# Rounds in groups of four, convolution four heads at a time, PSUM as one ring of single banks

## The chip, the core and the metric

One core of a Trainium2 chip runs the kernel as one launch. The metric is the device time in microseconds (us); three runs of the kernel before took 529.02 to 529.27 us, with a median of 529.07. The engines are called as in the profile: PE (TensorE, matmuls), PEld (its weight loads), DVE (VectorE), ACT (ScalarE), POOL (GpSimd) and SP (SyncE, here only an issuer of DMAs). In this kernel PE writes to PSUM, used as eight banks of 512 fp32 columns by 128 partitions, and results leave it through ACT or DVE.

## What is computed

```python
# x: (8, 3904, 192), weight: (8 heads, 7 taps)
w = softmax(weight, axis=-1)
x_pad = concat([zeros(8, 6, 192), x], axis=1)
conv[b, s, h, g] = sum_k w[h, k] * x_pad[b, s + k, h * 24 + g]
t = conv.reshape(31232, 192)
out = ((t @ w1) * (t @ w2)) @ w3 @ w_out     # 192 -> 1024 -> 1024 -> 192
```

## The kernel before, in words

The tokens are split into two streams of 15616 (four batches each, `r` = 0 and 1), which are worked on side by side: half of the 128 partitions holds stream 0, the other half stream 1. Work goes through three stages.

**Convolution** (`conv`, L261). Tokens come in windows of 64 rows, of which 58 are new; a *block* is a set of windows, `SIZES` = 10, 10, 10, 32, then five of 36 and one of 30. `load_x` (L89) brings a block to SBUF by POOL's DMAs. For each of eight heads four matmuls on quarters of the array (64x64, one for each half block and stream) multiply by a band matrix of the taps and write a pair of PSUM banks, one for each stream. DVE or ACT casts the pair to bf16 into `convo` (L295); heads 2 and 5 cross a border of 64 channels and take two casts. `store` (L299) writes the finished block to a DRAM buffer `rows` by SP's DMAs.

**First product** (`first_product`, L369). A *round* R is 512 tokens of each stream; there are 31, the last of them 256 wide. `transposes` (L345) brings a round from `rows` to SBUF, channels on partitions, with three transposing DMAs on SP, into `xT`, a ring of four rounds. For each of eight steps `ft` PE makes `pa` = t @ w1 and `pb` = t @ w2 for 128 of the 1024 columns, six matmuls of 64 rows by 512 columns each, which run two at a time; each fills a pair of banks. ACT casts `pa` to `asb` (L388), and DVE multiplies it with `pb` into `abT` (L389).

**Second product** (`second_product`, L394). W = w3 @ w_out is made once, in the prologue. For a round and a stream, 32 matmuls (four groups of 128 tokens, eight accumulation steps) multiply `abT` by W into one pair of banks `ops`; ACT copies it in one piece to `osb` (L410), one of five buffers of the tag `slot`, and SP issues the output DMA (L414).

PSUM is a pool of four tiles of two banks each (`banks`, L66), handed out in turn. The order on each engine is the order of the program text (`manual_schedule`): each engine and each DMA queue takes its instructions in that order and waits where data or a buffer isn't ready. SP's queue holds the stores, the transposes and the outputs in one line.

The prologue (up to L519) makes the weights, convolves blocks 0 to 3, runs the first products of rounds 0 to 2, and issues the transposes of rounds 3 to 6 (L515). Then come *phases* (L522): phase 0 has no first product, each later one has two rounds of them, and then second products trail: phase p does those of two rounds that were finished earlier (`LAG` = 2). Each phase convolves half a block of four heads in two places, two heads after its first second product and two at its end, and then sends the transposes of two more rounds:

```python
for i in range(done, last):
    second_product(i, 0)
    if b < NB and i == done:
        conv_two(b, 4 * e, (V, V))
    second_product(i, 1, i == NR - 1)
done = last
if b < NB:
    conv_two(b, 4 * e + 2, (V, V))
send(min(NR - 1, LAG + 2 * p + 4))
```

The last phase makes the first products of rounds 29 and 30 and all second products that are left.

Of the kernel before, what the change touches and what calls it, by code (L numbers as in the profile page):

```python
# [8 lines left out]
FP32 = mybir.dt.float32  # L9
# [7 lines left out]
def kernel(  # L17
# [19 lines left out]
    NS = 2  # L37
    TS = B * S // NS
    CH = 512
    NR = -(-TS // CH)  # L40
    RING = 4 * CH
    LAG = 2
    Q = 64
    ST = Q - PAD
    NP = D // Q
# [13 lines left out]
    const = ctx.enter_context(tc.tile_pool(name="const", bufs=1))  # L59
    stage = ctx.enter_context(tc.tile_pool(name="stage", bufs=2))  # L60
    work = ctx.enter_context(tc.tile_pool(name="work", bufs=2))
    psum = ctx.enter_context(tc.tile_pool(name="psum", bufs=4, space=bass.MemoryType.PSUM))
    dram = ctx.enter_context(tc.tile_pool(name="dram", bufs=1, space=bass.MemoryType.DRAM))
    ctx.enter_context(tc.manual_schedule())

    def banks(name):  # L66
        return psum.tile([128, NS, CH], FP32, tag="banks", name=name)

    def banks_bf16(name):
        return psum.tile([128, 16, 128], BF16, tag="banks", name=name)  # L70

    def slot(shape, dtype, name):
        return stage.tile(shape, dtype, tag="slot", bufs=5, name=name)
# [15 lines left out]
    def load_x(b, parts=(0, 1), streams=(0, 1)):  # L89
        tiles = xb_of.setdefault(b, [])  # L90
        zeros_of = zero_rows.setdefault(b, [])
        for i0, n in [v for e, v in enumerate(halves_of(b)) if e in parts]:
            if i0 == 0 and tiles:
                xb = tiles[0][0]
            else:
                xb = work.tile([128, n, D], BF16, tag="xb", bufs=6, name="xb")
            w = 0
            if i0 == 0:
                if not tiles:
                    nc.vector.memset(xb[:, 0, :], 0.0)  # L100
                for r in streams:
                    nc.gpsimd.dma_start(out=xb[Q * r:Q * r + Q, 1:n, :], in_=x_spans(r, 1, n - 1))  # L102
                w = n
            while w < n:
                i = i0 + w
                m = min(n - w, WB - i % WB)
                at_end = i + m == NWIN
                if at_end:
                    m -= 1
                if m:  # L110
                    for r in range(NS):
                        nc.gpsimd.dma_start(out=xb[Q * r:Q * r + Q, w:w + m, :],  # L112
                                            in_=x_spans(r, i, m))
                if i % WB == 0:
                    zeros_of += [(xb, 0, w), (xb, 1, w)]
                w += m
                if at_end:
                    nc.gpsimd.memset(xb[Q:128, w, :], 0.0)
                    t = tok(NWIN - 1) - PAD
                    nc.gpsimd.dma_start(out=xb[0:Q, w, :], in_=x_rows[t:t + Q, :])  # L120
                    nc.gpsimd.dma_start(out=xb[Q:Q + PAD + LAST, w, :],
                                        in_=x_rows[TS + t:TS + t + PAD + LAST, :])
                    w += 1
            if tiles and i0 == 0:
                continue
            if len(halves_of(b)) == 1:
                tiles += [(xb, 0), (xb, SIZES[b] // 2)]
            else:
                tiles.append((xb, 0))
# [61 lines left out]
    load_w(WC[1], WC[3])  # L191

    def warm(n, t=None):
        t = banks("warm") if t is None else t
        for j in range(n):
            nc.tensor.matmul(t[:, j % 2, :], zeros[:, 0:128], zeros, start=True, stop=True)  # L196

# [12 lines left out]
    nc.vector.reciprocal(out=wsum, in_=wsum)  # L210
    nc.vector.tensor_tensor(
        out=wrow, in0=wall, in1=wsum.unsqueeze(2).to_broadcast([1, H, K]), op=ALU.mult)
    wbc = banks("wbc")
    wbc = wbc[:, 0, 0:H * K // 2].rearrange("p (g e k) -> p g e k", g=2, e=2)
    wrow = wrow.rearrange("p (g a e) k -> p g a e k", g=2, a=2)
    for a in range(2):
# [20 lines left out]
        return c  # L237

    def band_sum(g, c, f):
        bps = banks("bps")  # L240
        for v, lhsT in enumerate((ident, swapped)):
            out = bps[:, 0, v * 128:v * 128 + 128].rearrange("p (e s) -> p e s", e=2)
            for k in range(K):
                nc.tensor.matmul(out, lhsT, c[:, :, k, :], start=(k == 0), stop=(k == K - 1))
        f(out=Aband[:, g].rearrange("p v e s -> p (v e s)"), in_=bps[:, 0, 0:256])
# [12 lines left out]
            c0, n = c0 + m, n - m  # L258
        return out

    def conv(b, h0, nh, evict=None, lead=0):  # L261
        n = SIZES[b] // 2
        if h0 == 0:
            convo_of[b] = work.tile([128, n, NP, NS, Q], BF16, tag="convo", bufs=2, name="convo")
        convo = convo_of[b]
        cps = banks("cps")
        warm(lead, cps)
        wd = nh * G

# [20 lines left out]
            del xb_of[b]  # L290
        if evict == ():
            return moves
        for e, (dst, part) in enumerate(moves):
            f = evict or [nc.scalar.copy]
            f[e % len(f)](out=dst, in_=part)  # L295
# [28 lines left out]
    def pe_transpose(b, k, lead=0):  # L324
        n = SIZES[b] // 2
        convo = convo_of[b]
        tps = banks_bf16("tps")
        for w in range(lead):
            nc.tensor.transpose(out=tps[:, w % 2, :], in_=zeros[:, 0:128], identity=ident)
        for w in range(n):  # L330
            nc.tensor.transpose(  # L331
                out=tps[:, w, :],
                in_=convo[:, w, k].rearrange("p r g -> p (r g)"), identity=ident)
        t0 = tok(FIRST[b])
        dst = xT[k][:, t0:t0 + 2 * n * ST].rearrange("p (c w s) -> p c w s", c=2, w=n)
        src = tps[:, 0:n, :].rearrange("p w (c s) -> p c w s", c=2)
        return dst, src[:, :, :, 0:ST]
# [30 lines left out]

    def first_product(R, between=None):  # L369
        N = width(R)  # L370
        ab = work.tile([128, JT, NS, CH], BF16, tag="abT", bufs=LAG + 1, name="abT")
        abT_of[R] = ab
        r0 = (R * CH) % RING
        for ft in range(JT):
            pq = []
            for i in range(2):
                p = banks("pa" if i == 0 else "pb")
                pq.append(p)
                for k in range(NP):
                    for r in range(NS):  # L380
# [10 lines left out]
            if between and ft in between:  # L391
                between[ft]()

    def second_product(R, r, split=False):  # L394
        ab = abT_of[R]
        ng = width(R) // 128
        t0 = r * TS + R * CH
        parts = [(g, g + 1) for g in range(ng)] if split else [(0, ng)]
        for e, (g0, g1) in enumerate(parts):
            m = g1 - g0  # L400
            ops = banks("ops")
            for g in range(m):
                for jt in range(JT):
                    nc.tensor.matmul(  # L404
                        ops[:, g // 2, (g % 2) * D:(g % 2) * D + D],
                        ab[:, jt, r, (g0 + g) * 128:(g0 + g + 1) * 128], W_sb[:, jt, :],
                        start=(jt == 0), stop=(jt == JT - 1))
            osb = slot([128, m, D], FP32, "osb")
            n = min(m, 2)
            (nc.vector.tensor_copy if split and e == 0 else nc.scalar.copy)(  # L410
                out=osb.rearrange("p (a g) d -> p a (g d)", g=n),
                in_=ops[:, 0:m // n, 0:n * D])
            t = t0 + g0 * 128
            (nc.scalar if split and g1 == ng else nc.sync).dma_start(  # L414
                out=out[t:t + m * 128, :].rearrange("(g p) d -> p g d", p=128), in_=osb)
        if r == 1:
            del abT_of[R]

# [13 lines left out]

    def w3_transpose(jt, f):
        w3b = w3b_of.pop(jt)
        tps = banks_bf16("w3ps")
        for gt in range(JT):
            nc.tensor.transpose(out=tps[:, gt, :], in_=w3b[:, gt * 128:(gt + 1) * 128],  # L437
                                identity=ident)
# [2 lines left out]

    def w3_product(jt):
        w3T = w3T_of.pop(jt)
        wps = banks("wps")
        for gt in range(JT):
            nc.tensor.matmul(wps[:, 0, 0:D], w3T[:, gt, :], wo_b[:, gt, :],  # L446
                             start=(gt == 0), stop=(gt == JT - 1))
# [48 lines left out]
        5: seq((pe_transposes, 2), (store, 2, 26))})  # L496
    first_product(2)

    def conv_two(b, h, engines):
        for j, f in enumerate(engines):  # L500
            conv(b, h + j, 1, (f,))
        if h + 2 == H:
            store(b)

    def send(last):
        while sent[0] <= last and min((sent[0] + 1) * CH, TS) <= stored[0]:
            transposes(sent[0])
            sent[0] += 1

    for jt in range(JT):  # L510
# [1 line left out]
        if 2 <= jt < 6:  # L512
            conv_two(3, 2 * (jt - 2), (V, A))
        if jt == 5:
            send(LAG + 4)  # L515
        if jt > 1:
            w3_product(jt - 2)
    w3_product(JT - 2)
    w3_product(JT - 1)  # L519


    phases = [()] + [(R, R + 1) for R in range(LAG + 1, NR, 2)]  # L522
    assert phases[-1][-1] == NR - 1
    pace = const.tile([1, 2], BF16)
    done = 0
    for p, rounds in enumerate(phases):
        b, e = PROLOGUE_BLOCKS + p // 2, p % 2
        if b < NB:
            for xb, r, w in zero_rows.pop(b, []):
                nc.gpsimd.memset(xb[Q * r:Q * r + PAD, w, :], 0.0)  # L530
        for j, R in enumerate(rounds):
            first_product(R)
            if j == 0 and b + 1 < NB:
                P(out=pace, in_=abT_of[R][0:1, JT - 1, 1, 0:2])  # L534
                load_x(b + 1, (0, 1) if p == 1 else (e,))
        last = NR if p == len(phases) - 1 else done + 2
        for i in range(done, last):
            second_product(i, 0)
            if b < NB and i == done:
                conv_two(b, 4 * e, (V, V))  # L540
            second_product(i, 1, i == NR - 1)
        done = last
        if b < NB:
            conv_two(b, 4 * e + 2, (V, V))
        send(min(NR - 1, LAG + 2 * p + 4))
    assert sent[0] == NR


# [28 lines left out]
```

## Time and profile before

| what | value |
|---|---|
| median of three runs | 529.07 us (529.02 to 529.27) |
| profiled execution, span from first to last instruction | 527.4 us |
| the median less that span | 1.67 us |
| granted TensorE clock | 1.000 |
| busy: PE, PEld | 519.1 us, 347.8 us |
| busy: DVE, ACT, POOL | 361.2 us, 319.0 us, 53.6 us |
| multiply into abT (L389), 128x1024 | 240 times, 1221 ns |
| cast to asb (L388), 128x1024 | 240 times, 1012 ns |
| copy to osb (L410), 128x768 | 60 times, 800 ns |
| cast of a conv head (L295), 128x864 | 30 times, 1052 ns |
| matmuls: first product, second product, conv | 2976, 1952, 320 |
| HBM | 129 GB/s over the span |

The profile names no time of the profiled execution other than its span; what the timed runs have over it is kept as a constant. A group's row has its line, engine and operation, what it writes and reads, its count, its busy time and the mean of one in ns, and then the idle time of its engine ahead of it with what ended it. A row of the timeline has start and length in us. Matmuls are pipelined: the length of one (376 ns for 512 columns) is longer than the distance from one to the next, so rates are read from the starts.

### The profile page before, as it was taken

Reading aid. Unit: us, or ns where it says so; the run is one execution under the profiler, and the core shown is the slowest. Engines: PE = TensorE matmul, PEld = TensorE weight load, DVE = VectorE, ACT = ScalarE, POOL = GpSimd, SP = SyncE. Lnnn points to the kernel's source line nnn. Section 1 sums busy time; section 2 is a strip of 40 time slices with the busy share of each in tenths; the row PEclk is TensorE's granted clock in tenths of the full one; section 3 lists DMA queues with packets and bytes.
Section 4 is the critical chain, followed back from the end, with each engine's and each line's share of the span. In section 5 each row is a group of like instructions: output and inputs, shape, how many; then the busy total and the mean of one; then the engine's idle time right before and its main releaser. Section 6 shows DMA issues by size and latency. Waiting matters only on the chain.

```text
span 527.4 us, 12699 instructions
## 1 busy us (share of the span) xinstructions
PE 519.1 (98%) x5459; PEld 347.8 (66%) x5459; DVE 361.2 (68%) x346; ACT 319.0 (60%) x356; POOL 53.6 (10%) x97
## 2 busy tenths in 40 slices
PE   7899999999999999999999999999999999999997
PEld 4455975857658576585765857658575574856777
DVE  6679459397593975939669496694957849377370
ACT  6787557375573755737557374673746647476562
POOL 8841002001010100201001010020000000000000
PEclk9999999999999999999999999999999999999999
DMA  8999449979472796637956369553735046240304
GB/s 120 140 205 182 106 95 183 194 164 143 132 90 91 173 138 131 88 103 149 148 140 78 117 146 128 147 59 123 149 80 134 1 139 131 71 106 2 121 2 150
DMA packets 130862, 63.28 MB, mean 120 GB/s; under 512 B 83290, under 2 KB 129782, under 8 KB 130806
## 3 DMA queue, kind: packets, MB, share of 16 engines
q1 hardware_dynamic: 92084, 45.95, 36.0%
q0 software_dynamic: 38576, 16.43, 26.7%
q8 instruction: 42, 0.69, 0.5%
q14 instruction: 14, 0.11, 0.1%
q10 hardware_dynamic: 146, 0.10, 0.1%
HBM read 33.25 MB, written 34.82 MB: 129 GB/s over the span
## 4 chain that ended last, share of the span: by engine, by line
PE 94%; POOL 1%; DMA 1%; DVE 1%; ACT 1%; issue 0%; POOLq 0%; ACTq 0%
PE ops L404 31%; PE pa L382 29%; PE pb L382 29%; PE cps L278 3%; DMA xb<-in_x_dram 1%; DVE abT L389 1%; PE wps L446 1%; ACT asb L388 1%; PE w3ps L437 0%; PE tps L331 0%; POOL wn L183 0%; POOL identw L166 0%; POOL xb L102 0%; POOL xb L135 0%; POOL xb L112 0%
## 5 line engine op out<-in xcount | busy, mean ns | idle before, releaser
L389 DVE TENSOR_TENSOR abT<-asb,pb 128x1024 bf16<-128x1024 bf16 (+1 forms) x248 | 298.1, 1204 | 45.9 <-ACT asb L388 29.8
L388 ACT CAST asb<-pa 128x1024 bf16<-128x1024 f32 (+1 forms) x248 | 247.6, 999 | 70.7 <-PE pa L382 69.9
L382 PE MATMUL pb<-xT,wn 64*128 64x512 bf16 (+1 forms) x744 | 201.4, 372 | 0.2
L382 PE MATMUL pa<-xT,wn 64*128 64x512 bf16 (+1 forms) x744 | 198.1, 373 | 0.6 <-DVE abT L389 0.3
L382 PE MATMUL pa<-xT,ws 64*128 64x512 bf16 (+1 forms) x744 | 198.2, 373 | 0.0
L382 PE MATMUL pb<-xT,ws 64*128 64x512 bf16 (+1 forms) x744 | 194.2, 373 | 0.0
L382 PEld LDWEIGHTS <-wn 64*128 64x128 bf16 x1488 | 138.6, 94 | 80.4 <-issue 4.6
L382 PEld LDWEIGHTS <-ws 64*128 64x128 bf16 x1488 | 129.0, 94 | 69.6 <-issue 4.0
L404 PEld LDWEIGHTS <-abT 128*128 128x128 bf16 x1952 | 159.7, 98 | 9.7 <-issue 9.7
L404 PE MATMUL ops<-W_sb,abT 128*128 128x192 bf16 x1952 | 165.7, 246 | 0.0
L410 ACT COPY osb<-ops 128x768 f32<-128x768 f32 (+2 forms) x62 | 48.8, 787 | 127.0 <-PE ops L404 127.0
L295 DVE CAST convo<-cps 128x864 bf16<-128x864 f32 (+7 forms) x65 | 52.0, 847 | 98.3 <-PE cps L278 98.3
L112 POOL DMA_DIRECT2D xb<-in_x_dram x38 | 29.9, 797 | 12.2 <-DMA w3b<-in_moe_w_dram 4.8
L534 POOL COPY pace<-abT 1x2 bf16<-1x2 bf16 x9 | 1.6, 175 | 268.1 <-DVE abT L389 268.1
L278 PE MATMUL cps<-xb,Aband 64*64 64x432 bf16 (+3 forms) x320 | 18.0, 309 | 1.6 <-DMA xb<-in_x_dram 1.5
L278 PEld LDWEIGHTS <-Aband 64*64 64x64 bf16 x320 | 6.0, 105 | 7.9 <-issue 7.0
L295 ACT CAST convo<-cps 128x640 bf16<-128x640 f32 (+4 forms) x13 | 7.4, 606 | 2.5 <-PE cps L278 2.5
L410 DVE COPY osb<-ops 128x192 f32<-128x192 f32 x1 | 0.4, 358 | 11.8 <-PE ops L404 11.8
L446 PE MATMUL wps<-wo_b,w3T 128*128 128x192 bf16 x64 | 6.3, 246 | 0.1
L446 PEld LDWEIGHTS <-w3T 128*128 128x128 bf16 x64 | 5.1, 98 | 1.0 <-issue 1.0
L196 PE MATMUL warm<-zeros 128*128 128x512 bf16 x8 | 3.7, 616 | 1.3 <-DVE ones L157 1.3
L361 POOL COPY ws<-wn 64x256 bf16<-64x256 bf16 x12 | 4.7, 395 | 0.7 <-DMA wn<-in_moe_w_dram 0.2
(54 smaller groups left out, 66.1 us busy)
## 6 DMA issues: line engine op xcount, KB each, us to landing
out_dram<-osb SPq DMA_DIRECT2D x60, 384.0 KB, 2.7
xb<-in_x_dram POOLq DMA_DIRECT2D x14, 432.0 KB, 8.6
rows<-convo SPq DMA_DIRECT2D x7, 648.0 KB, 9.3
xb<-in_x_dram POOLq DMA_DIRECT2D x8, 384.0 KB, 10.8
w3b<-in_moe_w_dram POOLq DMA_DIRECT2D x8, 256.0 KB, 8.7
rows<-convo SPq DMA_DIRECT2D x3, 576.0 KB, 5.6
xT<-rows SPq DMA_TRANSPOSE x84, 2.8
rows<-convo SPq DMA_DIRECT2D x2, 540.0 KB, 8.8
```

Source lines behind the costliest of these rows:

```text
L112: nc.gpsimd.dma_start(out=xb[Q * r:Q * r + Q, w:w + m, :], in_=x_spans(r, i, m))
L196: nc.tensor.matmul(t[:, j % 2, :], zeros[:, 0:128], zeros, start=True, stop=True)
L278: nc.tensor.matmul(view(slice(Q * c, Q * c + Q), r)[:, :, j * G:(j + 1) * G], band_of(h, r), xb[Q * r:Q * r + Q, w0:w0 + n, h * G:(h + 1) ...
L295: f[e % len(f)](out=dst, in_=part)
L361: f(out=wsw[k][d:d + Q, cs], in_=wn[k][e:e + Q, cs])
L382: nc.tensor.matmul(p[:, r, 0:N], w_of(i, k, r)[rs, ft * 128:(ft + 1) * 128], xT[k][rs, r0:r0 + N], start=(k == 0), stop=(k == NP - 1))
L388: nc.scalar.copy(out=asb[:, :, 0:N], in_=pa[:, :, 0:N])
L389: nc.vector.tensor_tensor(out=ab[:, ft, :, 0:N], in0=asb[:, :, 0:N], in1=pb[:, :, 0:N], op=ALU.mult)
L404: nc.tensor.matmul(ops[:, g // 2, (g % 2) * D:(g % 2) * D + D], ab[:, jt, r, (g0 + g) * 128:(g0 + g + 1) * 128], W_sb[:, jt, :], start=(jt ...
L410: (nc.vector.tensor_copy if split and e == 0 else nc.scalar.copy)(out=osb.rearrange("p (a g) d -> p a (g d)", g=n), in_=ops[:, 0:m // n, 0 ...
L446: nc.tensor.matmul(wps[:, 0, 0:D], w3T[:, gt, :], wo_b[:, gt, :], start=(gt == 0), stop=(gt == JT - 1))
L534: P(out=pace, in_=abT_of[R][0:1, JT - 1, 1, 0:2])
```

## The change

Phases become *groups*: group 0 has the second products of rounds 0 to 2, each later group four first products in a row and then the eight second products of the same four rounds. The last group takes round 30 ahead of rounds 27 to 29 in its first products. A whole block is convolved in each group, four heads after the second of its second products and four after the fourth (group 0) or fifth. PSUM becomes one tile of eight banks that are handed out singly; a second product takes one bank for two groups of tokens and is copied in two pieces into one `osb`, with one output DMA as before. The first head of each four is cast in two pieces, one for each bank. The transposes of round R+4 follow the first product of round R; a block's x is loaded in the group that convolves it, and has five buffers instead of six.

```diff
-    LAG = 2
+    GROUP = 4
+    FIRST_GROUP = 3
...
-    def banks(name):
-        return psum.tile([128, NS, CH], FP32, tag="banks", name=name)
+    NBANK = 8
+    ring = psum.tile([128, NBANK, CH], FP32, name="ring")
+    taken = [0]
+
+    def banks(n=NS):
+        b = taken[0] % NBANK
+        assert b + n <= NBANK
+        taken[0] += n
+        return ring[:, b:b + n, :]
...
-                xb = work.tile([128, n, D], BF16, tag="xb", bufs=6, name="xb")
+                xb = work.tile([128, n, D], BF16, tag="xb", bufs=5, name="xb")
...
+        if split:
+            moves = [(d[:, r], m[:, r]) for d, m in moves for r in range(NS)]
...
-        ab = work.tile([128, JT, NS, CH], BF16, tag="abT", bufs=LAG + 1, name="abT")
+        ab = work.tile([128, JT, NS, CH], BF16, tag="abT", bufs=GROUP, name="abT")
...
-    def second_product(R, r, split=False):
+    def second_product(R, r, last=False):
...
+        per = 1 if last else 2
+        osb = slot([128, ng, D], FP32, "osb")
+        for g0 in range(0, ng, per):
+            ops = banks(1)[:, 0, :]
+            for g in range(g0, g0 + per):
...
+            f = nc.vector.tensor_copy if last and g0 == 0 else nc.scalar.copy
+            f(out=osb[:, g0:g0 + per, :].rearrange("p g d -> p (g d)"), in_=ops[:, 0:per * D])
...
+    def conv_heads(b, heads):
+        for h in heads:
+            conv(b, h, 1, (V,), split=(h == heads[0]))
+        if heads[-1] == H - 1:
+            store(b)
...
-    phases = [()] + [(R, R + 1) for R in range(LAG + 1, NR, 2)]
-    assert phases[-1][-1] == NR - 1
+    groups = [list(range(FIRST_GROUP))]
+    groups += [list(range(R, R + GROUP)) for R in range(FIRST_GROUP, NR, GROUP)]
+    assert groups[-1][-1] == NR - 1
     pace = const.tile([1, 2], BF16)
...
+    for p, rounds in enumerate(groups):
+        b = PROLOGUE_BLOCKS + p
+        order = rounds[-1:] + rounds[:-1] if rounds[-1] == NR - 1 else rounds
+        for j, R in enumerate(order if p else ()):
+            first_product(R)
+            send(R + GROUP)
+            if j < 2 and b < NB:
+                P(out=pace, in_=abT_of[R][0:1, JT - 1, 1, 0:2])
+                load_x(b, (j,))
         if b < NB:
             for xb, r, w in zero_rows.pop(b, []):
                 nc.gpsimd.memset(xb[Q * r:Q * r + PAD, w, :], 0.0)
...
+        slots = {1: range(0, H // 2), len(rounds): range(H // 2, H)}
+        for i, (R, r) in enumerate((R, r) for R in rounds for r in range(NS)):
+            second_product(R, r, R == NR - 1 and r == 1)
+            if i in slots and b < NB:
+                conv_heads(b, slots[i])
```

## The prediction

> **What bounds the kernel now.** I read the page's busy rows first, then its chain, then the timeline of TensorE from stage to stage, and last SP's queue.
>
> ```profile
> PE 519.1 (98%) x5459; PEld 347.8 (66%) x5459; DVE 361.2 (68%) x346; ACT 319.0 (60%) x356; POOL 53.6 (10%) x97
> PE 94%; POOL 1%; DMA 1%; DVE 1%; ACT 1%; issue 0%; POOLq 0%; ACTq 0%
> ```
>
> PE holds the chain for 94% of the span. The change adds and removes no matmul, so it can win only what lies between PE's stages, and lose only by making PE wait. The pure rates come from long stretches without a seam: 13 steps of ft from 108.23 to 125.07 us in the chain in order of time give 1.295 us a step, and 128 second-product matmuls took 10.66 us, 2.665 for the 32 of one second product. The seams are in this piece of the timeline (start, length):
>
> ```profile
> 125.65 2.81 PE L404 MATMUL ops<-W_sb,abT 128*128 128x192 bf16 x32
> 128.39 0.56 PE L278 MATMUL cps<-xb,Aband 64*64 64x432 bf16 x8
> 128.50 0.80 ACT L410 COPY osb<-ops 128x768 f32<-128x768 f32 x1 [2.38 <-PE ops L404]
> 128.88 2.81 PE L404 MATMUL ops<-W_sb,abT 128*128 128x192 bf16 x32
> 128.90 2.02 DVE L295 CAST convo<-cps 128x864 bf16<-128x864 f32 x2 [1.53 <-PE cps L278]
> ```
>
> A cluster of two heads holds PE from 128.39 to 128.88, 0.49 us. A narrow window splits it: the four matmuls of head one start at 128.39, those of head two at 128.60, so a head costs 0.21 and leaving the cluster 0.28 after the last head's start. ACT starts 0.11 after the cluster's start, DVE 0.51 after (0.43 in the next cluster). With 0.05 for entering it, a cluster of two costs 0.54.
>
> The row that decides is in SP's queue, which issues in program order:
>
> ```profile
> 57.40 5.48 SPq L321 DMA_DIRECT2D rows<-convo  x4
> 63.89 17.68 SPq L349 DMA_TRANSPOSE xT<-rows  x12
> 81.67 23.89 SPq L414 DMA_DIRECT2D out_dram<-osb  x8
> ```
>
> The transposes of rounds 3 to 6 occupy the queue from 63.89 to 81.57, and the first output block, ready in SBUF at 63.93, leaves at 81.67. The DMA view of 81.6 to 82.9 alone, where that one transfer is issued, gives its landing:
>
> ```profile
> out_dram<-osb SPq DMA_DIRECT2D x1, 384.0 KB, 3.7
> ```
>
> So it lands at 85.4. Today nobody waits for that: this phase makes four blocks (osb), there are five buffers, and the sixth block comes at about 99.
>
> **The change, step by step.** Terms are made on the profiled span of 527.4 us; the timed runs have a median of 529.07, and I keep the 1.67 between as it is.
>
> *(1) Group 0: six second products before any first product.* PE starts them at 60.29 as now. Six at 2.665 and two conv clusters at 1.17 (step 2) end at about 78.7. The sixth block takes the slot buffer of the first, and in the built program its first ACT copy waits for the first output's DMA. PE has that copy's bank ready at 77.3; the DMA lands at 85.4, since the twelve transposes stand ahead of it in SP's queue in both programs. Behind that copy on ACT, in order, are the block's second copy and all casts asb of round 3. PE goes on: pa, pb, pa of round 3 find free banks (0.648 each, to 80.65); the second pb needs the sixth block's two banks. ACT copies them 85.4 to 86.4 (0.48 each, by the one 128x384 copy in the trace); PE gets its bank at 86.0. The first cast runs 86.4 to 87.4 (1.01), the first multiply to 88.6 (1.22), and PE's third pb, which needs the bank of that multiply, starts at 88.65 instead of 81.9. After that a step costs DVE 1.22 to 1.27 and PE 1.295, so nothing more is lost and nothing is caught up: **+6.7**. By the shortest and longest landing of all outputs (1.7 and 4.6) it is +4.7 to +7.6.
>
> *(2) Conv four heads at a time.* Four heads take all eight banks. Without a wait the cluster is 4 x 0.21 + 0.07 + 0.05 = 0.96. Two waits are new. Head four needs the banks of the second product just ended: ACT starts at +0.11, 0.48 for the copy, so +0.64 against head four's own +0.63: nothing. The next second product needs the first bank of head one, which DVE empties: start +0.47, half a head (432 elements) for which the trace has no row:
>
> ```profile
> L295 DVE CAST convo<-cps 128x576 bf16<-128x576 f32 x10 | 7.5, 753 | 32.1 <-PE cps L278 32.1
> L295 DVE CAST convo<-cps 128x288 bf16<-128x288 f32 x10 | 4.5, 447 | 0.0
> ```
>
> The line through both gives 600 ns; 753 and 447 are its bounds. With 0.05 from DVE's end to PE (105.66 + 1.05 ended, PE started at 106.76) the bank is free at +1.12 instead of the +0.91 without a wait. Later banks are in time: DVE needs 0.97 a head, PE takes 2.67 over two banks. So a cluster costs 1.17: 12 x 1.17 against 24 x 0.54 is **+1.1** (no DVE wait: -1.4; the 753 row: +2.9).
>
> *(3) Fewer seams.* From the last pb pair (125.34 + 0.216) to the second product (125.65) is 0.09; 14 such seams become 7: -0.6. Twelve first products now start right behind a conv cluster, and DVE's casts hold up their second pb: the phases' first halves are 20.90 and 20.95 where 16 steps are 20.73, of which 0.09 is the seam, so 0.08 to 0.13 each, gone: -1.2. Together **-1.8** (-1.2 to -2.2).
>
> *(4) The half round, 30.* It goes behind round 29 now, where the casts and multiplies of wide steps still run:
>
> ```profile
> 504.55 0.27 PE L382 MATMUL pa<-xT,wn 64*128 64x256 bf16 x1
> ...
> 511.04 2.65 PE L404 MATMUL ops<-W_sb,abT 128*128 128x192 bf16 x30
> ```
>
> 6.49 us for 96 matmuls that need 5.18 (6 x 0.108 x 8); 0.09 is the seam. Moved ahead of round 27 it starts with DVE idle; DVE's 0.68 a step against PE's 0.65 costs 0.3: **-0.9** (-1.2 to 0).
>
> *(5) At nothing.* Two ACT copies of 0.48 for one of 0.80: ACT is idle between (2.38 before a copy), a bank lasts 1.33. Transposes of round R+4 right behind round R: some 4 us of SP, needed over 23 us later; the outputs behind them wait up to 4 us, and outside group 0 a sixth block comes 17 us into its stage. The store in mid-stage: its readers come over 18 us later. x loads in the same group: the second is issued about 22 us into it and takes 13.2 at most, conv reads at 47. Five xb buffers: the prologue's last two loads wait for conv of blocks 0 and 1, long done. If one of these covers fails, PE waits by the lack.
>
> Sum: 6.7 + 1.1 - 1.8 - 0.9 = +5.1; span 532.5, time **534.2**.
>
> **Rivals.**
> *A, the clock gate.* In step 1 PE idles from 80.65 to 86.0. At the program's start, after idleness, five 512-column matmuls took 2.32 us with a 0.6 tail, 0.43 apart, where later ones go at 0.216, and the slow spell was over by 5.6 us. Were it so again from 86.0, the two pairs before 88.65 are covered, and of the rest some 2 us at half speed cost about +1: 535.2. The longest idle time of PE behind that in the waits is 1.2 us, so this trace cannot tell. Beside it: the Trainium skill, "TensorE: Matmul & The Clock Gate" (HAM oscillation), says that PE idle for longer than about 3.4 us falls back to half clock until it has been busy as long; by that the +1 is more likely than not, and no run here shows it yet.
> *B, faster: the output comes in time.* The third pb is late by the landing less 78.7, so from a landing by 78.7 on step 1 costs nothing, and the gain of steps 2 to 4 is left: 529.07 - 1.6 = 527.5. It needs the twelve transposes at the shortest of all 84 (1.13 each, 13.6 without gaps, from 63.89) and the output at the shortest of all (1.7): that lands at 79.2, late by 0.5, and the conv clusters or seams must give that back. Against: 17.68 and 3.7 at this very place, and nothing ahead of it in the queue changes.
> *C, a short wait:* a landing between 79.2 and 81.3, which is late by 0.5 to 2.6: 528.0 to 530.1.
> *D, conv clusters at their dear end* (half a head at 753 ns), with step 1 as forecast: +1.8 more, 536.0. For it: the shape is new. Against: casts of 480 elements took 653.
> *E, the ring isn't one of single banks* and PE waits for the whole ring: the built program has one wait per bank or pair, for ACT or DVE, as before, so hardly; it would cost a cast a step, hundreds of us. I leave it out.
>
> **How the numbers follow.** Forecast 0.5, A 0.27, D 0.11, B 0.06, C 0.06. The likeliest is 534.2. Range: down to +4.7 with the other steps at -2.6 (531.2), up to A and D together with a little (537.0). 0.2% (1.06 us) is about what a measurement can tell here: faster (below 528.0) is B, 0.06; same is C, 0.06; slower is the rest, 0.88.
>
> **What would show it.** In the changed trace: ACT idle for 8 to 9 us before a copy osb, up to about 85.4 and released by an output DMA, and PE idle about 5 us from 80.6, the only wait of that size. Conv clusters from 0.9 (no DVE wait) to 1.3 from their start to the next second product. The first products of a group behind the start seam at 1.295 a step without a late second pb. Round 30 in about 5.5. If PE has no gap near 80, step 1 is wrong and B holds; if the steps after the gap are at 2.6 instead of 1.3, A holds.

## The result, and the profile after

The changed kernel takes **538.08 us** in the median of four runs (537.72 to 539.35), the kernel before in the same session 529.06: a ratio of 1.0174 with a 95% interval of 1.016 to 1.0189. That is 9.0 us slower. The forecast was 5.1 us slower, 534.2, and the range ended at 537.0. The profiled execution took 537.88, its span is 536.2, so the 1.67 between span and time still holds. The difference of the spans is 8.7 us (536.15 less 527.44), and that is what is explained below.

The page's busy rows and its chain, then the clock row of the 40 slices:

```profile
PE 519.4 (97%) x5459; PEld 356.2 (66%) x5459; DVE 361.8 (67%) x358; ACT 328.1 (61%) x416; POOL 53.7 (10%) x98
...
PEclk9999997999999999999999999999999999999999
...
PE 85%; DVE 1%; DMA 1%; SPq 0%; issue 0%; ACT 0%; ACTq 0%; DVEq 0%
```

PE has the same matmuls and the same busy time, so the 8.7 us are idle time or a slower clock. The clock row has a single dent, the 7 in slice seven (80.4 to 93.8 us): look there first. SP's queue there, by its timeline:

```profile
58.69 5.55 SPq L331 DMA_DIRECT2D rows<-convo  x4
65.29 18.46 SPq L359 DMA_TRANSPOSE xT<-rows  x12
83.84 3.16 SPq L425 DMA_DIRECT2D out_dram<-osb  x4
```

The first output still stands behind the twelve transposes and leaves at 83.84. The chain goes right through it:

```profile
80.19 2.07 PE ring L392 x18
...
82.54 1.21 SPq L359
...
83.84 2.84 DMA out_dram<-osb
...
86.78 0.49 ACT osb L419
...
87.31 42.76 PE ring L392 x366
```

Read it downwards: three first-product tiles of round 3, then a transpose on SP, the output DMA, ACT's copy into the buffer that this DMA freed, and only then PE again. The timeline of ACT and then that of PE say the same from the other side; the bracket holds the idle time and what ended it:

```profile
77.58 0.48 ACT L419 COPY osb<-ring 128x384 f32<-128x384 f32 x1 [0.84 <-PE ring L414]
86.78 0.86 ACT L419 COPY osb<-ring 128x384 f32<-128x384 f32 x2 [8.72 <-DMA out_dram<-osb]
87.52 1.95 ACT L398 CAST asb<-ring 128x1024 bf16<-128x1024 f32 x2
```

```profile
81.86 0.38 PE L392 MATMUL ring<-xT,ws 64*128 64x512 bf16 x1
87.31 0.58 PE L392 MATMUL ring<-xT,wn 64*128 64x512 bf16 x1 [5.08 <-ACT osb L419]
87.69 0.62 PE L392 MATMUL ring<-xT,ws 64*128 64x512 bf16 x2
88.07 0.63 PE L392 MATMUL ring<-xT,wn 64*128 64x512 bf16 x1
```

Behind the gap the matmuls start some 0.4 us apart, where 0.216 was usual. The table by stretches has PE's busy time third from the left (after the stretch and its length) and the granted clock third from the right:

```profile
82.00:84.00 2.00, 0.23 (x4) 0.00 (x0) 0.00 (x0) 0.00 (x0) 0.00 (x0) 1.00 0.34 76
84.00:86.00 2.00, 0.00 (x0) 0.00 (x0) 0.00 (x0) 0.00 (x0) 0.00 (x0) 1.00 0.78 213
86.00:88.00 2.00, 0.69 (x3) 0.24 (x4) 0.00 (x0) 1.22 (x3) 0.00 (x0) 0.60 0.97 319
88.00:90.00 2.00, 2.00 (x12) 0.84 (x10) 1.41 (x2) 1.47 (x2) 0.00 (x0) 0.50 0.97 314
90.00:92.00 2.00, 2.00 (x13) 0.93 (x10) 1.15 (x2) 1.01 (x1) 0.00 (x0) 0.50 0.72 169
92.00:94.00 2.00, 2.00 (x16) 1.08 (x14) 1.01 (x1) 1.00 (x1) 0.00 (x0) 0.69 0.88 176
```

So both the wait of step 1 and the clock of rival A came. Finer stretches put the fall at 86.4 and the return at 93.2: 6.8 us at half clock.

The starts of PE's stages, before against after, show what else moved:

| stretch | before | after |
|---|---|---|
| program start to first second product | 60.29 | 61.73 |
| first products of rounds 3 to 6 | 20.97 + 20.90 | **49.88** |
| first products of four later rounds | 41.66 to 41.87 | 41.55 |
| conv cluster, start to next second product | 0.49 (two heads) | 1.13 and 1.08 (four heads) |
| eight second products and their conv | 23.50 | 23.62 |
| first products of the last four rounds (30 half) | 37.69 | 36.99 |
| last ACT copy's start to the span's end | 2.95 | 3.52 |

The row in bold is 8.3 us over the one below it in the same kernel. The first row, +1.44, was forecast as no change.

### The profile page after: what moved, and what is told of

It reads as the page before. It is cut to its first block, busy times and chain, and to the rows that moved or that the text cites. A ratio compares the mean times of both kernels' runs of the same rounds, so it can differ in the third digit from the quotient of the medians.

```text
span 536.2 us, 12829 instructions
## 1 busy us (share of the span) xinstructions
PE 519.4 (97%) x5459; PEld 356.2 (66%) x5459; DVE 361.8 (67%) x358; ACT 328.1 (61%) x416; POOL 53.7 (10%) x98
## 4 chain that ended last, share of the span: by engine, by line
PE 85%; DVE 1%; DMA 1%; SPq 0%; issue 0%; ACT 0%; ACTq 0%; DVEq 0%
PE ring L392 54%; PE ring L414 30%; DVE convo L305 1%; PE ring L286 1%; DMA out_dram<-osb 1%; PE ring L457 1%; DMA xT<-rows 0%; SPq L359 0%; ACT osb L419 0%; DVE abT L399 0%; PE ring L448 0%; ACTq L419 0%; SPq L425 0%; DVEq L305 0%
## 5 line engine op out<-in xcount | busy, mean ns | idle before, releaser
L399 DVE TENSOR_TENSOR abT<-asb,ring 128x1024 bf16<-128x1024 bf16 (+1 forms) x248 | 298.1, 1204 | 90.1 <-ACT asb L398 52.3
L392 PE MATMUL ring<-xT,wn 64*128 64x512 bf16 (+1 forms) x1488 | 321.7, 375 | 7.8 <-ACT osb L419 5.1
L392 PE MATMUL ring<-xT,ws 64*128 64x512 bf16 (+1 forms) x1488 | 321.1, 375 | 0.1
L398 ACT CAST asb<-ring 128x1024 bf16<-128x1024 f32 (+1 forms) x248 | 247.5, 999 | 70.9 <-PE ring L392 70.4
L414 PE MATMUL ring<-W_sb,abT 128*128 128x192 bf16 x1952 | 164.3, 246 | 1.1 <-DVE convo L305 0.2
L419 ACT COPY osb<-ring 128x384 f32<-128x384 f32 x122 | 58.1, 477 | 125.7 <-PE ring L414 106.7
L305 DVE CAST convo<-ring 128x432 bf16<-128x432 f32 (+7 forms) x77 | 51.6, 737 | 56.0 <-PE ring L286 51.9
L286 PE MATMUL ring<-xb,Aband 64*64 64x432 bf16 (+3 forms) x320 | 16.4, 306 | 0.9 <-DMA xb<-in_x_dram 0.6
L305 ACT CAST convo<-ring 128x640 bf16<-128x640 f32 (+4 forms) x13 | 7.4, 606 | 2.1 <-PE ring L286 2.1
L457 PE MATMUL ring<-wo_b,w3T 128*128 128x192 bf16 x64 | 6.3, 246 | 0.1
```

Of the source, the lines that this page charges most:

```text
L286: nc.tensor.matmul(view(slice(Q * c, Q * c + Q), r)[:, :, j * G:(j + 1) * G], band_of(h, r), xb[Q * r:Q * r + Q, w0:w0 + n, h * G:(h + 1) ...
L392: nc.tensor.matmul(p[:, r, 0:N], w_of(i, k, r)[rs, ft * 128:(ft + 1) * 128], xT[k][rs, r0:r0 + N], start=(k == 0), stop=(k == NP - 1))
L398: nc.scalar.copy(out=asb[:, :, 0:N], in_=pa[:, :, 0:N])
L399: nc.vector.tensor_tensor(out=ab[:, ft, :, 0:N], in0=asb[:, :, 0:N], in1=pb[:, :, 0:N], op=ALU.mult)
L414: nc.tensor.matmul(ops[:, (g - g0) * D:(g - g0) * D + D], ab[:, jt, r, g * 128:(g + 1) * 128], W_sb[:, jt, :], start=(jt == 0), stop=(jt = ...
L419: f(out=osb[:, g0:g0 + per, :].rearrange("p g d -> p (g d)"), in_=ops[:, 0:per * D])
```

## The experiments

The theory after the result: the wait for the sixth buffer costs about 6.4 and the clock behind it about 2; without both, the kernel stands at about 529.7, because 1.4 that the change loses in the prologue eats what it gains later. Rivals: the wait comes from the ring or the larger conv clusters and not from the buffer; the slow clock is free; the prologue's loss is chance. The spans are compared stage by stage with *six blocks* (the first experiment), which is the changed kernel without its gap.

**Six buffers for the output blocks.**

```diff
-        return stage.tile(shape, dtype, tag="slot", bufs=5, name=name)
+        return stage.tile(shape, dtype, tag="slot", bufs=6, name=name)
```

> The changed kernel with six output buffers instead of five. Theory (the sixth block's copy waits for the first output DMA, which stands behind twelve transposes; the PE gap that follows lets the clock drop): no ACT wait for an output near 78 us, no PE gap near 82, granted clock 1.000, group 1's first products in 41.6 us instead of 50.0; 538.1 - 8.4 = 529.7. What then remains against before is +1.4 in the prologue, -1.6 at the seams and about +0.7 in the last DMA. Rival (round 3 is held by something else, such as its transposes, and the buffer is only the first thing to be seen): the gap stays or moves, 533 to 538.

Measured: 529.48 (529.02 to 531.86), ratio 1.0013 [1.0002, 1.0023], span 527.9. The first products of rounds 3 to 6 take 41.55 like all others, although the transposes still occupy SP's queue for 18.5 us and the output leaves at 83.93. ACT copies the sixth block without a wait for a DMA and goes on to the casts:

```profile
78.93 0.48 ACT L419 COPY osb<-ring 128x384 f32<-128x384 f32 x1 [0.84 <-PE ring L414]
80.25 0.48 ACT L419 COPY osb<-ring 128x384 f32<-128x384 f32 x1 [0.84 <-PE ring L414]
81.01 1.01 ACT L398 CAST asb<-ring 128x1024 bf16<-128x1024 f32 x1 [0.28 <-PE ring L392]
```

One buffer removes 8.3 us of span, so wait and slow clock together are that one buffer's price. What is left of the change is 0.4 us over the kernel before, 0.1 to 1.2 by the interval.

**PE kept busy during the wait.** 24 matmuls on zeros go into the bank pair that round 3's first product is about to overwrite; ACT's wait stays.

```diff
+                if ft == 0 and i == 0:
+                    warm(lead, p)
...
+        busy = 24 if p == 1 else 0
...
+            first_product(R, lead=busy if j == 0 else 0)
```

> The changed kernel with 24 matmuls on zeros ahead of round 3's first product (24 x 0.216 = 5.2 us), so that PE works through the wait, which stays. Theory (of the 8.4 us some 6.4 are the wait itself and 2.0 the half clock after it): ACT waits for the output as before, the clock stays at 1.0 in 86 to 94 us, and the time is 538.1 - 2.0 = 536.1. Rival (the half clock is covered by the refilling of ACT and DVE, which start late in any case): unchanged, 537.5 to 538.5.

Measured: 536.4 (535.58 to 538.02), ratio 1.0143 [1.0129, 1.0157], span 534.2. The zero matmuls of its PE timeline, ACT's copy of the sixth block, and two stretches:

```profile
80.03 5.34 PE L204 MATMUL ring<-zeros 128*128 128x512 bf16 x24
```

```profile
86.89 0.86 ACT L421 COPY osb<-ring 128x384 f32<-128x384 f32 x2 [8.81 <-PE ring L394]
```

```profile
86.00:88.00 2.00, 1.99 (x17) 0.75 (x15) 0.00 (x0) 1.11 (x3) 0.00 (x0) 1.00 0.97 322
88.00:90.00 2.00, 1.46 (x13) 0.45 (x11) 1.30 (x2) 2.00 (x3) 0.00 (x0) 1.00 0.98 320
```

The copy starts as late as in the changed kernel (86.78). The bracket names PE, whose matmuls run all through this time, but the copy also waits for the output, issued at 83.97, and the last of that transfer's semaphore updates comes at 86.79. The clock stays at 1.00. From the first second product of group 0 to that of group 1 it takes 66.54 us, in the changed kernel 68.27 (61.73 to 130.00), with six buffers 59.93 (61.76 to 121.69). This splits the 8.3: **6.6 are the wait, 1.7 the slow clock**. The spans give 6.3 and 2.0, since the tail of this one execution is 0.2 shorter, and the medians of the times 6.9 and 1.7, so the split is good to some 0.3. PE ran 5.9 us at half clock, from 87.31 to 93.24, which alone would cost 3.0. But with the clock at 1.00 PE still waited for a multiply until 89.97, so only the 3.3 us behind that count, 1.6 at half speed.

**The transposes spread between the outputs.** Five buffers; the transposes of rounds 4, 5 and 6 each go behind one of the first three outputs.

```diff
-            send(FIRST_GROUP + GROUP - 1)
+            send(FIRST_GROUP)
...
+            if p == 0 and i < 3:
+                transposes(sent[0])
+                sent[0] += 1
```

> The changed kernel, five buffers, but the transposes of rounds 4, 5 and 6 go into SP's queue one round behind each of the first three outputs instead of ahead of all. Theory (the place in SP's queue is the cause): the first output is issued near 69 us and lands near 72, the sixth block finds its buffer free, the same 529.7 as with six buffers. Rival (the output lands late for its own sake, with the queue's DMAs slow at that time): still an ACT wait of some us, 532 to 538.

Measured: 529.33 (528.99 to 532.34), ratio 1.0009 [0.9994, 1.0024], span 527.6. Its SP queue:

```profile
65.31 5.40 SPq L359 DMA_TRANSPOSE xT<-rows  x3
70.75 0.91 SPq L425 DMA_DIRECT2D out_dram<-osb  x1
71.70 3.98 SPq L359 DMA_TRANSPOSE xT<-rows  x3
```

The output leaves 13 us earlier, the gap is gone with five buffers. So the cause has two halves, either of which can be taken away: a sixth block this early, and an output behind twelve transposes.

**The kernel before, with six second products in phase 0.** Pool, conv of two heads and five buffers stay as they were.

```diff
-        last = NR if p == len(phases) - 1 else done + 2
+        last = NR if p == len(phases) - 1 else done + (3 if p == 0 else 2)
```

> The kernel before with one edit: phase 0 makes all six second products of rounds 0 to 2 (as the change does), the later phases go on from there. Pool of pairs, five buffers and conv two heads at a time stay. Theory (the loss needs only a sixth block ahead of the first output's landing, not the ring or the conv): PE idle for about 5 us near 80 us, the granted clock at 0.5 behind it for some 6 us, time 529.05 + 8 to 9 = 537 to 538.5. Rival (the ring's single banks or the clusters of four are needed for the wait): no gap, 528.5 to 529.5. Rival two (gap, but no gate): 535.5.

Measured: 538.27 (537.96 to 539.39), ratio 1.0167 [1.0142, 1.0192]. First PE's waits (us in total, times, longest), then three stretches:

```profile
PE pb L382 <- ACT osb L410: 6.3, 1, 6.3
```

```profile
82.00:84.00 2.00, 0.00 (x0) 0.00 (x0) 0.00 (x0) 0.00 (x0) 0.00 (x0) 0.83 0.33 70
84.00:86.00 2.00, 0.00 (x0) 0.00 (x0) 0.00 (x0) 0.00 (x0) 0.00 (x0) 0.50 0.85 269
86.00:88.00 2.00, 1.10 (x6) 0.50 (x7) 0.20 (x1) 1.95 (x3) 0.00 (x0) 0.50 0.98 319
```

One number in the old kernel brings the whole loss, wait and clock. The ring of single banks and the clusters of four are not needed for it.

**One pair of banks skipped after the prologue's transposes.** The prologue's loss shows in PE's timeline after, and not in that of the kernel before:

```profile
24.46 0.37 PE L392 MATMUL ring<-xT,wn 64*128 64x512 bf16 x1 [0.58 <-DVE abT L399]
...
36.69 0.37 PE L392 MATMUL ring<-xT,wn 64*128 64x512 bf16 x1 [0.63 <-DVE abT L399]
```

```profile
24.00 0.37 PE L382 MATMUL pa<-xT,wn 64*128 64x512 bf16 x1
```

Both waits stand right behind three tiles that PE transposes (`pe_transposes`, L349). In the built program before, the pool gives the next `pa` a pair that ACT has emptied, so its tiles aren't handed out strictly in turn, as is said above; its `pa` starts at 24.00, while DVE's multiplies of the `pb` ahead run until 24.54. The counter of the ring gives the next pair in turn, which DVE has yet to read for a multiply. With six buffers, one pair is passed over:

```diff
         pairs = [pe_transpose(b, k) for k in range(NP)]
+        banks()
```

> Six buffers, and in the prologue one pair of banks is skipped after each group of three transposing tiles, so that the next pa takes a pair that ACT has emptied rather than the last one that DVE has still to empty. Theory (the 1.4 us that the prologue lost come from the ring's order, by two waits of PE for DVE of 0.6 us right behind the transposes, near 24.5 and 36.7 us, and what follows): second products start near 60.4 instead of 61.7 us; 529.7 - 1.3 = 528.4. Rival (the prologue is late through its first loads, which came up to 0.9 us later in that profile): no change against six buffers alone, 529.7.

Measured: 529.06 (528.68 to 531.34), ratio 1.0009 [1.0, 1.0018]; second products start at 61.64. A miss: the start was expected at 60.4. The stretches between PE's transposes became only 0.28 shorter each; a wait of 0.2 for DVE appears one tile later. The start is so little earlier also because this execution was 0.46 behind at the first of the two places already (transposes at 23.15 against 22.69). This neither shows nor refutes the order as the cause.

**The old order of the pairs.** With six buffers, the four pairs are handed out after the transposes so that ACT, DVE and ACT emptied the first three, as before.

```diff
+    turn = [0, 1, 2, 3]
...
+        b = 2 * turn[taken[0] // 2 % 4] + taken[0] % 2
...
+        i = taken[0] // 2
+        last, *t = [turn[(i + j) % 4] for j in range(4)]
+        for j, v in enumerate((t[0], last, t[2], t[1])):
+            turn[(i + j) % 4] = v
```

> Six blocks as in e1_six_blocks, and the four pairs of the ring are handed out in another order from the last transposing tiles of the prologue on, so that the first product of round 2 meets pairs that ACT, DVE and ACT emptied, as in the kernel before. Theory (the prologue's 1.4 us come from the order in which a plain counter hands out the pairs): second products start at about 60.5 instead of 61.75, time 528.2 to 528.4. Rival (it is the layout as one tile, or loads that arrive late, and the order does nothing): start at 61.6 to 61.8, time 529.3 to 529.5.

Measured: 528.23 (527.29 to 530.86), ratio 0.9978 [0.9962, 0.9994], second products from 60.51. The same place in its PE timeline, with no wait:

```profile
23.87 0.37 PE L397 MATMUL ring<-xT,wn 64*128 64x512 bf16 x1
```

1.25 of the prologue's 1.44 are the order of the pairs; the layout as one tile is unchanged in this version. It isn't chance: over all traces second products start at 61.35 to 61.86 in the eight versions with the plain counter, at 60.51 to 60.99 in the three with the old order (this one and the last two below), and at 60.29 and 60.64 in the two with the pool.

**No cast in halves.** With six buffers, the first head of a cluster is cast whole.

```diff
-            conv(b, h, 1, (V,), split=(h == heads[0]))
+            conv(b, h, 1, (V,))
```

> e1_six_blocks without the cast of the first head in halves. Theory (the first bank of the cluster sets when PE goes on): the second product behind a cluster waits for a whole cast of 1.05 instead of about 0.6, so a cluster takes about 1.55 from start to start instead of 1.11, and 12 of them cost +4 to +5: 533.5 to 534.5. Rival (the second product waits for ACT's copies or for PE itself): no change, 529.3 to 529.7.

Measured: 535.36 (534.99 to 535.89), ratio 1.012 [1.0105, 1.0135]; a cluster takes 1.62 and 1.54. PE's waits name it:

```profile
PE ring L414 <- DVE convo L305: 6.6, 12, 0.7
```

Twelve clusters, twelve waits. The span is 5.6 longer, which is 12 x 0.46; the time lies 0.9 above the 533.5 to 534.5 expected. In the changed kernel the half cast ends this wait at 1.08 to 1.13.

**Clusters of 3, 3 and 2 heads**, six buffers, no cast in halves:

```diff
-        slots = {1: range(0, H // 2), len(rounds): range(H // 2, H)}
+        slots = dict(zip((1, 3, 5) if p else (1, 2, 4), (range(0, 3), range(3, 6), range(6, 8))))
```

> e1_six_blocks with the heads of a block in clusters of 3, 3 and 2, without the cast in halves. A cluster of three leaves two banks free, so the second product behind it waits for no DVE cast. Theory: a cluster of three costs 0.75 and one of two 0.54, 2.04 a block against 2 x 1.13 = 2.26, and no bank is waited for: -1 to -1.3 us in six blocks, time about 528.3. Rival (DVE's casts of whole heads, 1.05 each, make a later second product wait for a bank instead): no change or slower, 529.4 to 530.5.

Measured: 528.12 (527.62 to 529.46), ratio 0.9975 [0.9962, 0.9987]. A cluster of three in its PE timeline, then one of four in that of *six blocks*:

```profile
126.78 0.74 PE L286 MATMUL ring<-xb,Aband 64*64 64x432 bf16 x12
127.45 1.25 PE L414 MATMUL ring<-W_sb,abT 128*128 128x192 bf16 x13
```

```profile
127.07 1.01 PE L286 MATMUL ring<-xb,Aband 64*64 64x432 bf16 x16
128.21 1.48 PE L414 MATMUL ring<-W_sb,abT 128*128 128x192 bf16 x16
```

0.67 for three heads, 1.14 for four: the fourth costs 0.47 and not 0.21, as it leaves no free bank. A block's second products and conv take 23.38 instead of 23.62.

**Two heads at four places**, six buffers, no cast in halves:

```diff
+        slots = {i: range(2 * j, 2 * j + 2) for j, i in enumerate((0, 2, 4, 6) if p else (0, 1, 3, 4))}
```

> e1_six_blocks with the convolution of two heads at four places of a group instead of four heads at two, and no cast in halves. Theory (a cluster of four costs 1.13 from start to start beyond nothing else, two clusters of two cost 2 x 0.54 = 1.08 less what the extra seams hide): the 12 clusters of four and 24 of two differ by little, -0.5 to -0.9 us at most, time 528.6 to 529.0. Rival (the four-head cluster is what costs the gain, because its casts hold up later banks too): -2 us or more, 527.5 or below.

Measured: 529.51 (529.09 to 530.04), ratio 0.9996 [0.9985, 1.0008]; the same as *six blocks*, so neither reading held. The clusters are cheap (0.49), but a second product that stands alone takes 2.75 where two in a row take 5.38, and a block comes to 23.61. The number of heads in a cluster is worth little between two and four; three is the best of them.

**Round 30 behind round 29 again**, six buffers:

```diff
-        order = rounds[-1:] + rounds[:-1] if rounds[-1] == NR - 1 else rounds
+        order = rounds
```

> e1_six_blocks with round 30 behind round 29 again, as in the kernel before. Theory (a half round behind wide rounds pays for their casts and multiplies, ahead of them for the 0.69 of a narrow multiply against 0.65 of PE): the first products of the last group take 0.5 to 0.7 more, time about 530.0. Rival (it is worth the 0.9 that the prediction gave it): 530.4. Rival two (its place is worth nothing): 529.4.

Measured: 530.4 (530.07 to 533.21), ratio 1.0032 [1.0019, 1.0045]. The last group's first products take 37.87 instead of 37.00. The place is worth 0.87, which is the prediction's figure and not the smaller one that was expected here.

**All that helped, together:** six buffers, the old order of pairs, clusters of 3, 3 and 2.

> Three edits at once: six blocks (e1_six_blocks), the pairs of the prologue in the old order (e5_ring_order), heads in clusters of 3, 3 and 2 (e7_three_heads). Theory (three separate costs, which add up): 529.5 - 1.2 - 1.3 = 527.0, within 526.7 to 527.5, which is faster than the kernel before by 2 us; second products start at 60.5 and a group behind group 0 takes 64.93 from first product to first product. Rival (the edits share a limit, a conv or a DMA that becomes late when the prologue is shorter): 528 or more.

Measured: 527.16 (526.39 to 529.74), ratio 0.9968 [0.9957, 0.9979]: 1.9 us faster than the kernel before. A group takes 64.93 from first product to first product, as expected. In its profiled execution second products start at 60.99, half a us late, with a wait of 0.89 for a multiply at 16.0 us, ahead of the place that the order changes.

**The same, with the last copies in two buffers.** The very last second product's two pieces get a buffer each, as in the kernel before.

```diff
-        osb = slot([128, ng, D], FP32, "osb")
+        osb = None if last else slot([128, ng, D], FP32, "osb")
...
+            o = slot([128, 1, D], FP32, "osb") if last else osb[:, g0:g0 + per, :]
```

> e9_all with the very last second product's two copies written to two buffers, as in the kernel before, instead of two parts of one. The end of the span came 3.4 to 3.6 us after the last ACT copy's start in all versions with one buffer and 2.9 in the kernel before. Theory (the shared buffer delays the last transfer): 0.6 less than e9_all, about 526.4, and 2.9 from that copy to the end. Rival (it is the transfers in flight beside it, or chance): the same as e9_all, 3.4 to 3.6.

Measured: 526.95 (526.77 to 528.24), ratio 0.9963 [0.9951, 0.9975]; from the last copy to the end 3.61, so the shared buffer isn't why the tail is longer. Against the version above the 0.2 is within both intervals.

## Why the prediction was off

By its own steps, in us of span; the wait and the clock are from the first two experiments, step 4 from *round 30 behind round 29 again*, the rest from stage starts.

| step | forecast | measured |
|---|---|---|
| 1, wait for the first output | +6.7 (4.7 to 7.6) | +6.6 |
| A, half clock behind it | +1, as a rival of 0.27 | **+1.7**, and it came |
| 2, conv of four heads | +1.1 | +0.7 |
| 3, fewer seams | -1.8 | -1.5 |
| 4, round 30 moved | -0.9 | -0.87 |
| 5 and "as now": the prologue | 0 | **+1.4** |
| 5: the tail | 0 | +0.6 |
| sum | +5.1, without A | +8.6 of 8.7 |

**Step 1 was right, with its mechanism, place and size.** The output left 2.2 later than forecast (83.84, of which 1.4 are the prologue) and landed faster (2.84 against 3.7); PE's gap was 5.1 where 5.35 were forecast. That the size fits to 0.1 is luck in part: the transposes took 0.8 longer than before and the landing 0.9 less than forecast, and the two cancel. *Six blocks*, the spread queue and the edit of the old kernel each show that it needs both the early sixth block and the twelve transposes.

**The size and the chance of A failed.** The step that failed is "of the rest some 2 us at half speed cost about +1". It took the length of the slow spell from the program's start, where the slow matmuls, from 1.3 us on, were over by 5.6. Here the clock was at half for 6.8 us, 5.9 of them with matmuls. The point up to which the prediction held the slow clock covered, the start of the third pb, forecast at 88.65, is at 89.97 with PE kept busy, so 3.3 us were left instead of 2: 1.6 by this working, 1.7 measured. The mechanism was right, with its covered part; the length was not. Its chance was too low as well: that nothing in the trace before showed such a gap was no reason against it, and the same text held the +1 for more likely than not by the Trainium skill ("TensorE: Matmul & The Clock Gate", HAM oscillation), and yet gave A 0.27 against 0.5.

**"PE starts them at 60.29 as now" failed.** The prediction looked at the ring for one question only, in its rival E: whether waits are for banks or for the whole ring. It did not ask which engine empties the pair that is next. A plain counter in place of a pool can change that where tiles come in odd numbers, here behind three transposing tiles, twice, for 0.6 each. The old order of pairs gives 1.25 of the 1.44 back. About 0.2 is not accounted for by it; the first stretches of single executions vary by up to half a us, so it is left open.

**The tail was left out.** The prediction put it at nothing without a reason. From the last ACT copy to the end it takes 3.2 to 3.8 in every version of the change, and 2.9 to 3.0 in the kernel before and in its version with six second products. The shared buffer is excluded. The traces place the difference in the last output DMA: from its issue on ACT to the end of SP's wait for it there are 2.0 to 2.6 us in the versions of the change, 1.7 in the two others. Why it takes longer stays open.

Steps 2 to 4 came within 0.4 each. Their sum came out at the forecast's -1.6, as the errors of steps 2 and 3 cancel. (Step 3 is -1.7 in rounds 3 to 26 and +0.2 in the last four, which take 37.87 with round 30 in its old place against 37.69 before.) The gain is real: with the wait gone and the old order of pairs, the change is faster than the kernel before by 0.22% [0.06, 0.38].

## What to carry to other kernels

A buffer count is right only for a given order of work: when stages are regrouped, count again for each group which block is first to reuse a buffer, and look in the DMA queue for what stands ahead of the transfer that frees it. A wait of PE that lasts several us has a second price, the clock behind it (here 1.7 us behind a gap of 5.1); price both, or keep PE busy. When a pool becomes a counter, follow the turn through every place where the number of tiles is odd, and ask which engine has to empty the next one.

## What the runs showed of the hardware

The granted clock fell to 0.50 during both gaps of PE and stayed there for the same 6.8 us, wherever the matmuls came back. In the changed kernel the last matmul ended at 82.2, the clock fell at 86.4, matmuls went on at 87.3, and full clock was back at 93.2. In the old kernel with six second products these are 80.6, 83.3, 86.9 and 90.2. So the fall came 4.2 us after the last matmul in the one and 2.8 in the other, and full clock came back after 5.9 and 3.3 us of matmuls.

The Trainium skill, "TensorE: Matmul & The Clock Gate" (What's actually happening), says that activity is judged over windows of 3.41 us that run freely and don't begin with the kernel's own events. The two runs agree: 6.8 is two such windows, and the different delays fit windows that began at about 83.0 and 79.9. Counted so, a window with 0.65 us of matmuls at its start still led to the fall, one with 2.5 us was too little to end the slow spell, and one busy but for 0.15 us ended it. The prediction used the page's shorter form (idle longer than 3.4, then busy as long), from which neither 2.8 nor 6.8 would follow. The traces have a further sign that the windows are these. Their first entry of full clock, at the program's start, stands at 4.49 us in the changed kernel and at 4.83 in the other, and the falls at 86.41 and 83.34 come 81.92 and 78.51 us behind it, 24 and 23 times 3.413. Which share of a window has to be busy isn't shown beyond these few cases.
